# Windowed attention and a four-expert mixture in one schedule: rows of 512 bytes, weights in pieces, a third blocked group of batch 0, late rows through memory, and planner settings by phase

## The chip, the cores and the metric

The kernel runs on one core of one Trainium2 chip. The metric is the device time of one execution in microseconds, as a median of runs. The profile is of one further execution of the same program; its span goes from the first to the last instruction of the program.

The engines are named as in the profile: PE (TensorE, matrix products and, as PEld, weight loads), DVE (VectorE), ACT (ScalarE), POOL (GpSimd) and SP (SyncE). Each works through its own list of instructions in order. SP, ACT and POOL also issue transfers.

## The reference, cut to what matters

```python
# q, k, v: (4, 8, 768, 64) f32; n_sink 4, window 128
scores = q @ k.T / sqrt(64)
keep = (key < 4) | ((query - key >= 0) & (query - key < 128))
a = softmax(where(keep, scores, -1e9))
x = (a @ v) with the heads side by side        # (3072, 512)
# w1: (4, 512, 1024), w2: (4, 1024, 512), domain_probs: (3072, 4)
p = domain_probs / (domain_probs.sum(-1) + 1e-9)
out = sum over e of p[:, e] * (relu(x @ w1[e]) @ w2[e])   # (3072, 512) f32
```

So there is attention over a window of 128 keys and four sink keys, batch by batch, and behind it a mixture in which all four experts work on every token.

## The kernel before

**Units.** The 768 tokens of a batch are three groups `g` of 256. A unit is (batch `b`, group `g`, expert `e`). Attention of a group needs q and k with the head dimension on the partitions (`qkT`), scores per head pair (line 676, products of 64 rows), exponentials on ACT (702), masks on DVE (695, 711), the sinks' scores (637, 32 columns of weights at a time), the product with v (736, 743), a division (770 to 782) and a transpose into `xT`, on PE for batch 0 (801) and by a transfer on SP for the others (760).

**First product of a unit.** A slow unit has four steps of 8 products of 256 columns (1051); each needs a quarter of w1's columns. A fast unit does 7 block products instead of 8, each 8 products of 128 columns (1138), in the manner of Strassen and Winograd: DVE forms sums of weight blocks once per expert (`weight_form1`, 362) and of token blocks once per group (`tokens`, 1083), and per unit DVE adds two block results more than for a slow one (1191, 1206) and ACT copies two (1184, 1197). `START` says from which (batch, group) on an expert's units are fast. Results leave PSUM through relu for batch 0 (1064 to 1066, 1157 to 1159; the gate is applied after the second product), and through relu times gate on DVE for batches 1 to 3 (1075, 1171), which needs the gates spread over all partitions (`load_gate`, 453, a transfer on SP into one of `NGATE` = 5 buffers).

**Second product.** Batch 0's groups go through `emit_second` (1374): per half group and expert 8 products of 512 columns (1388), scaled and added by DVE (1398, 1400). The other nine groups, `PAIRS` (913), go by 7 block products for each of the four experts, summed over the experts in PSUM (`emit_product`, 1296; products of 256 columns at 1312), with block sums of the units' results formed by DVE (`chore`, 1215) and of w2 (`weight_form`, 326).

**Transfers in.** Batch 0's first group of q and k comes on SP and ACT as f32 (`load_first`, 254) and is cast (`cast_first`, 275). All other rows, v and the weights are cast by POOL's transfers: rows by `load_nat` (230; per 128 tokens one transfer of q and one of k, each with 1024 pieces of 256 bytes in memory) into `qkn` buffers, of which there are six; v by `load_v` (296), w1 by `load_w1` (306; expert 0 in two halves), w2 by `load_w2` (319). Batch 0 is turned on PE (`transposes`, 556), later batches by SP's transposing transfers (`turn_nat`, 241), six per batch, which can start when the scores of the batch before are done, since `qkT` has one buffer. `idle_products` (546) issues products of zeros where PE would stand idle.

**Order.** There is no scheduler at run time and none in the framework. The program's own planner sets the order while the kernel is built: it keeps a clock per engine in `t` (98), lists the steps that may come next with a time and a priority (main loop from 1446), emits the best, and keeps evictions in `pend` until their engine is due (`later`, `flush`, 142 to 165). The settings at lines 60 to 92 weigh the steps: `SHARE_OF`, `LEAD` and `DUE` how fast attention runs ahead of the mixture, `LOW_PRODUCT`, `LOW_SECOND`, `OPEN`, `EARLY` and `STEP0` the priorities, `GATE`, `FORM`, `TOKEN`, `MARGIN` and `MASK_SLACK` how long evictions and sums may wait, `PAIR` whether two scores steps go together, `FULL` and `WIDE` how many units are open. The transfers' place in their queues follows from the same loop (`loads`, `turns`).

```python
        opts.append((max(p, now), HIGH_PRODUCT if behind > BEHIND or mix.live >= FULL else LOW_PRODUCT, "product", None))
        opts += [(max(f, now), p, "first", x) for f, p, x in mix.firsts()]
        opts.append((max(s2, now), 1 if mix.since >= 1 else LOW_SECOND, "second", None))
        soonest = min(o[0] for o in opts)
        if soonest > now + 40 and flush(soonest, True):
            continue
        if soonest < 20000 and soonest > now + 220:
            idle_products(acc[1], 1, G)
            continue
```

The output is staged per group (`osb0`, `osb`, `osl`) and stored by SP. The last block product, P4 of the last group, is copied by ACT (1360) and stored by SP (1304).

Of the kernel before, what the change touches and what calls it, by code (L numbers as in the profile page):

```python
# [16 lines left out]
def kernel(  # L17
# [41 lines left out]

    NGATE = 5  # L60
    START = {0: (0, 2), 1: (0, 2), 2: (0, 0), 3: (2, 1)}
    MIX = 5
    SHARE_OF = (1.034, 1.037, 1.072)
    LEAD = (1.026, 0.9853)
    DUE = 1.356
    LOW_PRODUCT = 2.147
    LOW_SECOND = 2.509
    HIGH_PRODUCT = -1
    EARLY = 0.1973
    MASK_SLACK = 200.0  # L70
    GATE = 2639.0
    GATE0 = 6000.0
    FORM = 1000.0
    TOKEN = 4559.0
    MARGIN = 2117.0
    HOLD = 0
    FULL = 8
    STEP0 = 0.2923
    READY = 40
    WIDE = 3  # L80
    OPEN = 2.551
    ONACT = 1
    ONE = 2
    PAIR = 0
    BEHIND = 2351.0
    CHORES = 3
    OWN = 2
    LAST = 2
    BIASED = 1
# [8 lines left out]
    t = {"pe": 1200.0, "act": 0.0, "dve": 0.0, "pool": 1280.0, "sp": 800.0, "sw": 4800.0, "hw": 0.0}  # L98
    ring, whole = [0.0] * 6, [False] * 6
    WARM = 6600.0  # L100
    FLIP, LATE = 103.6, 500.0
# [79 lines left out]
    ROW = {64: 12.8, 128: 22.6, 512: 79.8, 1024: 156.2}  # L181

    def lands(key, rows, cols, *deps):
        issued = pool(0, *deps, fixed=880)
        at = max(t["sw"], issued + 1500)
        t["sw"] = at + rows * ROW[cols] / 16
        landed[key] = t["sw"] + 900 + (BACKLOG if key[0] == "w1" or backed else 0.0)
        if key[0] == "w1":
            backed.append(key)
        moved.append([key, at, t["sw"], ROW[cols]])  # L190

    moved, backed = [], []
    BACKLOG = 1300.0
    TURNED, SHARE = 66, 31.0

    def sp(*deps, issue=530, takes=600, turning=False):
        t["sp"] = max([t["sp"], *deps]) + issue
        at = max(t["hw"], t["sp"] + 800)
        row = next((x[3] for x in moved if x[1] <= at < x[2]), 0.0)
        if turning and row:  # L200
            t["hw"] = at + TURNED * (row + SHARE)
            t["sw"] += TURNED * SHARE
            for x in moved:
                if x[2] > at:
                    x[1] += TURNED * SHARE * (x[1] > at)
                    x[2] += TURNED * SHARE
                    landed[x[0]] = x[2] + 900 + BACKLOG * bool(backed)
                    if x[0][0] == "w1" and ("w1", x[0][1]) in landed:
                        landed["w1", x[0][1]] = max(landed["w1", x[0][1]], landed[x[0]])
        else:  # L210
            t["hw"] = at + takes + max(0.0, min(takes, t["sw"] - at)) * (not turning)
# [17 lines left out]

    def load_nat(b, tb):  # L230
        both = sb.tile([P, 2, H, D], BF16, name="qkn", tag="qkn", bufs=NQB)
# [9 lines left out]
    def turn_nat(b, tb):  # L241
# [8 lines left out]
        qkn_free.remove(1e12)  # L250
        qkn_free.append(turned_at[b, tb])
        qkn_free.sort()

    def load_first():

        raw = {name: mo.tile([P, 2, 4, 2 * D], FP32, name=f"{name}raw", tag=f"wide{i}", bufs=1) for i, name in enumerate("qk")}
        for half in range(2):
            hs = slice(4 * half, 4 * half + 4)
            for name, src in (("q", q), ("k", k)):
                x = raw[name][:, half]  # L260
                (nc.sync if name == "q" else nc.scalar).dma_start(
                    out=x, in_=src[0, hs, 0:G, :].rearrange("h (p t) d -> p h (t d)", t=2),
                )
                nat[0, half, name, "raw"] = x
            landed["first", half] = ((4870.0, 5180.0), (7550.0, 7350.0))[half]
# [5 lines left out]
    first = {name: sb.tile([P, 2, H, D], BF16, name="qkn", tag="qkn", bufs=NQB) for name in "qk"}  # L271
    qkn_free[-2:] = [1e12] * 2
    cast_at = {}

    def cast_first(half):
        hs = slice(4 * half, 4 * half + 4)

        def cast(at):
            cast_at[half] = at
# [1278 lines left out]
```

## Time and profile before

| | |
|---|---|
| runs | 361.69, 362.18 and 364.25 us; median 362.18 |
| profiled execution | 362.99 us, of which the span is 361.2 |
| PE, share of the span | 97% |
| weight loads | 82% |
| DVE | 82% |
| ACT, POOL | 46%, 19% |
| moved by transfers | 37.25 MB |
| POOL's queue (q0) | 77520 packets, 17.31 MB |
| SP's queue (q1) | 38668 packets, 18.75 MB |
| granted clock of PE | 1.00 |

The shares are busy time over the span. Busy intervals of consecutive instructions overlap, so a share near 100% says that the engine always had an instruction under way, not that it did its most. In the lines that follow, a group has busy time in us, the mean of one in ns, then the idle time before it and what ended that.

### The profile page before, as it was taken

The page shows a single profiled execution, that of the slowest core. Times are in us where ns is not written, and L with a number is a line of the kernel's source. Part 1 is how long each engine was busy: PE and PEld are TensorE (multiplying, and loading weights), DVE is VectorE, ACT ScalarE, POOL GpSimd, SP SyncE. Part 2 cuts the span into 40 slices and gives each one's busy share as a digit, 9 for nine tenths or more (in the row PEclk, how much of TensorE's full clock was granted, in tenths as well). Part 3 has the DMA queues.
Part 4 walks back from the last instruction along what each step waited for, and adds up shares of the span by engine and source line. Part 5 has one row for each costly group of instructions (what it writes and reads, how often), then busy time and mean ns, then how long its engine had stood idle before and what let it go on. Part 6 is the DMA issues. An engine that isn't in the chain of part 4 may idle for free.

```text
span 361.2 us, 10566 instructions
## 1 busy us (share of the span) xinstructions
PE 351.7 (97%) x4410; PEld 296.2 (82%) x4423; DVE 296.4 (82%) x671; ACT 164.9 (46%) x419; POOL 70.4 (19%) x90
## 2 busy tenths in 40 slices
PE   8799999998999999999999999999999999999996
PEld 3485767756668868898899899899999999999985
DVE  4665999868868979789789989979999998987840
ACT  5764634557754463655464465546222223212110
POOL 8935016223500616101440000000000000000000
PEclk9999999999999999999999999999999999999999
DMA  9999999999943999917899131214113102000011
GB/s 172 182 186 201 210 209 177 149 126 184 149 92 97 146 175 152 135 49 74 128 155 174 16 104 31 55 50 62 37 25 89 31 22 85 16 29 33 0 61 58
DMA packets 117292, 37.25 MB, mean 103 GB/s; under 512 B 100613, under 2 KB 112741, under 8 KB 117245
## 3 DMA queue, kind: packets, MB, share of 16 engines
q0 software_dynamic: 77520, 17.31, 56.1%
q1 hardware_dynamic: 38668, 18.75, 26.0%
q8 instruction: 34, 0.56, 0.6%
q10 hardware_dynamic: 1056, 0.52, 0.5%
q14 instruction: 14, 0.11, 0.2%
HBM read 40.45 MB, written 6.34 MB: 130 GB/s over the span
## 4 chain that ended last, share of the span: by engine, by line
PE 72%; DMA 21%; POOL 4%; issue 1%; DVE 1%; ACT 0%; SPq 0%
PE acc L1312 31%; PE cps L1138 27%; DMA w<-in_moe_w_dram 11%; PE hps L1051 6%; DMA qkn<-in_k_dram 4%; DMA vx<-in_v_dram 3%; PE acc L1388 3%; DMA xT<-onat 2%; PE sps L676 2%; PE od L743 2%; POOL qkn L233 1%; POOL vx L298 1%; PE od L736 1%; POOL w L311 1%; POOL w L321 0%
## 5 line engine op out<-in xcount | busy, mean ns | idle before, releaser
L1138 PEld LDWEIGHTS <-w 128*128 128x128 bf16 x1184 | 73.3, 98 | 3.7 <-issue 1.5
L1312 PEld LDWEIGHTS <-H 128*128 128x128 bf16 x600 | 56.0, 98 | 6.2 <-issue 0.6
L702 ACT ACTIVATE aT<-sps 128x512 bf16<-128x512 f32 (+1 forms) x96 | 47.4, 573 | 18.5 <-PE sps L676 18.5
L1171 DVE SCALAR_TENSOR_TENSOR H<-cps,gates 128x512 bf16<-128x512 f32 x78 | 52.9, 682 | 1.3 <-PE cps L1138 0.2
L1138 PEld LDWEIGHTS <-vf 128*128 128x128 bf16 x768 | 47.3, 98 | 1.7 <-issue 0.4
L1312 PE MATMUL acc<-w,H 128*128 128x256 bf16 x360 | 47.7, 273 | 0.0
L1138 PE MATMUL cps<-T,w 128*128 128x128 bf16 x592 | 45.1, 219 | 0.1
L1138 PE MATMUL cps<-xT,w 128*128 128x128 bf16 x592 | 44.8, 219 | 0.0
L1388 PE MATMUL acc<-w,H 128*128 128x512 bf16 x179 | 43.4, 379 | 1.0 <-issue 0.5
L782 ACT ACTIVATE onat<-od,R 128x64 bf16<-128x64 f32 x144 | 32.9, 324 | 23.9 <-DVE R L770 23.9
L1051 PE MATMUL hps<-xT,w 128*128 128x256 bf16 x352 | 43.5, 273 | 0.1
L1184 ACT COPY cps<-cps 128x512 f32<-128x512 f32 x37 | 21.4, 579 | 38.4 <-PE cps L1138 32.8
L1138 PE MATMUL cps<-T,vf 128*128 128x128 bf16 x512 | 38.3, 219 | 0.1
L1051 PEld LDWEIGHTS <-w 128*128 128x128 bf16 x352 | 32.9, 98 | 5.6 <-issue 1.3
L1388 PEld LDWEIGHTS <-H 128*128 128x128 bf16 x192 | 17.8, 98 | 17.9 <-issue 0.3
L298 POOL DMA_DIRECT2D vx<-in_v_dram x24 | 21.4, 901 | 48.8 <-PE od L743 44.8
L1312 PEld LDWEIGHTS <-S 128*128 128x128 bf16 x288 | 27.2, 98 | 2.9 <-issue 0.2
L1191 DVE TENSOR_TENSOR cps<-H,cps 128x512 f32<-128x512 f32 x31 | 21.4, 692 | 8.4 <-PE cps L1138 5.5
L1360 ACT COPY osb<-acc 128x256 f32<-128x256 f32 x28 | 10.5, 373 | 38.3 <-PE acc L1312 38.3
L1312 PE MATMUL acc<-wf,H 128*128 128x256 bf16 x184 | 25.8, 273 | 0.0
L695 DVE TENSOR_TENSOR aT<-aT,mask 128x1024 bf16<-128x1024 bf16 (+1 forms) x36 | 22.8, 640 | 1.9 <-ACT aT L702 1.7
L1206 DVE TENSOR_TENSOR H<-H,cps 128x512 f32<-128x512 f32 x31 | 21.2, 683 | 3.8 <-PE cps L1138 3.7
(126 smaller groups left out, 543.9 us busy)
## 6 DMA issues: line engine op xcount, KB each, us to landing
w<-in_moe_w_dram POOLq DMA_DIRECT2D x7, 1024.0 KB, 16.2
out_dram<-osb SPq DMA_DIRECT2D x19, 256.0 KB
gates<-gate_rows SPq DMA_DIRECT2D x36, 128.0 KB
vx<-in_v_dram POOLq DMA_DIRECT2D x24, 128.0 KB, 6.9
qkn<-in_q_dram POOLq DMA_DIRECT2D x22, 128.0 KB, 6.8
qkn<-in_k_dram POOLq DMA_DIRECT2D x22, 128.0 KB, 7.2
w<-in_moe_w_dram POOLq DMA_DIRECT2D x2, 512.0 KB, 9.0
out_dram<-osl SPq DMA_DIRECT2D x4, 256.0 KB
```

Of the source, the lines that this page charges most:

```text
L298: nc.gpsimd.dma_start(out=vx[tb][:, :, 0:D], in_=v[b, :, tb * P:(tb + 1) * P, :].rearrange("h p d -> p h d"),)
L695: nc.vector.tensor_mul(a, a, m[:, None, :].to_broadcast([P, 2, w]))
L702: nc.scalar.activation(out=a[:, ph], in_=sps[ph][:, 0:w], func=AF.Exp, scale=scale)
L782: nc.scalar.mul(o[:, qi, hp, ph * D:(ph + 1) * D], od[:, qi, ph, 0:D], R[:, qi, ph])
L1051: nc.tensor.matmul(h[:, i].rearrange("p (q n) -> p q n", q=2), lhsT=w1_sb[e][:, db, fb * P:(fb + 1) * P], rhs=xT[b, g][:, :, db], start=(i ...
L1138: nc.tensor.matmul(y[:, f], lhsT=A[:, d, f * P:(f + 1) * P], rhs=T[:, d], start=(m in ("P1", "P5") and f == 0 and d == 0), stop=(d == 1), ...
L1171: nc.vector.scalar_tensor_tensor(out=dst, in0=src, scalar=0.0, in1=gate, op0=ALU.max, op1=ALU.mult)
L1184: nc.scalar.copy(out=tiles["Y"], in_=y)
L1191: nc.vector.tensor_add(tiles["V"], c5, tiles["X"])
L1206: nc.vector.tensor_add(c5, c5, y)
L1312: nc.tensor.matmul(x, lhsT=self.operand(b, g, e, m)[:, f], rhs=forms[e][m][:, f], start=(k == 0 and f == 0 and m in (("P1", "P5", "P2") if ...
L1388: nc.tensor.matmul(op, lhsT=H[:, fb // QF, fb % QF, s], rhs=w2_sb[e][:, fb, :], start=(fb == 0), stop=(fb == NFB - 1),)
```

## The change

What it does, part by part:

- **Rows of 512 bytes.** Batch 0's groups 2 and 3 (`g` = 1, 2) are fetched with two neighbouring tokens per partition (`load_runs`), so that a piece in memory has 512 bytes; q and k of a group are one transfer each. The pairs are then regrouped by eight copies of 256 columns per group, q's on DVE and k's on ACT, in front of the transposes on PE; the copies out of PSUM put the tokens back in order. The first group's casts go by head pair instead of by half.
- **Weights in pieces.** Expert 0's w1 comes in quarters, and a step of the first product waits for its quarter alone; its w2 comes in two halves of 256 columns, and the second product with it goes by half columns.
- **Third group's second product in blocks.** Batch 0's third group joins `PAIRS`: its units are gated on eviction, like those of later batches, and it takes the 7 block products. For this the gate rows are made once the planner's clock passes `ROWS` and no longer when attention of batch 0 is done, and four more gates are loaded. The units of this group come in the order of the experts. `START` also moves: expert 0 is fast from batch 2 on instead of from batch 0's third group, expert 3 from (2, 0) instead of (2, 1).
- **Late rows through memory.** q and k of batches 2 and 3 are cast into a buffer in memory by POOL's transfers and turned from there by SP's, so that they need no `qkn` buffer.
- **Refitted by phase.** Most settings become four values, one for each stretch of the planner's clock (up to 60, 130 and 220 us, and behind), chosen by `by`. `PAIR` and `FORCE` can make scores steps wait for their partner.
- **Smaller ones.** The masks are built by other instructions and earlier, the zeros come first on DVE and the idle products ahead of the first rows are of 256 columns (13 written out, and more where the planner sees a wait), the sinks' v is loaded for batch 0 first, the last P4 is copied in halves by ACT and DVE and stored in halves by ACT and SP. The product of 512 columns that marks a fast unit's second PSUM bank as written (1144 to 1149) occurs twice in the new order and never in the old one.

The diff, cut to its core:

```diff
+    SPLIT = (60000.0, 130000.0, 220000.0)
-    START = {0: (0, 2), 1: (0, 2), 2: (0, 0), 3: (2, 1)}
+    START = {0: (2, 0), 1: (0, 2), 2: (0, 0), 3: (2, 0)}
-    SHARE_OF = (1.034, 1.037, 1.072)
-    LEAD = (1.026, 0.9853)
-    DUE = 1.356
+    SHARE_OF = (1.044, 0.95, 1.067)
+    LEAD = (1.012, 0.9701)
+    DUE = (1.063, 2.057, 1.149, 1.283)
-    GATE = 2639.0
+    GATE = (300.0, 1413.0, 1377.0, 471.2)
-    PAIR = 0
+    PAIR = (0, 1, 1, 1)
+    FORCE = (0, 0, 1, 1)
...
+    def by(x):
+        return x[sum(t["pe"] > at for at in SPLIT)]
...
     def load_nat(b, tb):
+        if b > 1:
+            if b not in turned_rows:
+                turned_rows[b] = dram.tile([S, 2, H, D], BF16, name=f"rows{b}")
+            x = nat[b, tb] = turned_rows[b][tb * P:(tb + 1) * P]
+            for i, src in enumerate((q, k)):
+                nc.gpsimd.dma_start(out=x[:, i], in_=src[b, :, tb * P:(tb + 1) * P, :].rearrange("h p d -> p h d"))
+                lands(("qk", b, tb), H * P, D)
+            return
...
+    def load_runs(g):
+        x = mo.tile([P, 2, H, 2, D], BF16, name="runs", tag="H" if g == 1 else "osb", bufs=NH if g == 1 else 1)
+        for i, src in enumerate((q, k)):
+            nc.gpsimd.dma_start(
+                out=x[:, i].rearrange("p h t d -> p h (t d)"),
+                in_=src[0, :, g * G:(g + 1) * G, :].rearrange("h (p t) d -> p h (t d)", t=2),
+            )
...
+        for hp in range(NHP):
+            part = join(2, lambda at, hp=hp: regrouped.__setitem__((g, hp), at))
+            for i, engine in enumerate(("dve", "act")):
+                def run(engine, i=i, h=2 * hp, part=part):
+                    copy(engine, rows[i][:, :, h:h + 2], x[:, i, h:h + 2].rearrange("p h t d -> p t h d"))
+                    part(clock(engine, 4 * D, rate=1.3))
+                later(engine, landed["qk", 0, g], 200 * hp, run)
...
-        nc.gpsimd.dma_start(out=w2_sb[e], in_=moe_w2[e].rearrange("(fb p) d -> p fb d", p=P))
+        for c in halves(e):
+            nc.gpsimd.dma_start(
+                out=w2_sb[e][:, :, c], in_=moe_w2[e][:, c].rearrange("(fb p) d -> p fb d", p=P),
+            )
...
-    for tb in (2, 3):
-        load_nat(0, tb)
-    load_v(0, (2, 3))
-    load_w1(0, 2, [0])
-    load_w1(0, 2, [1])
+    load_runs(1)
+    if not VPOS:
+        load_v(0, (2, 3))
+    load_w1(0, QF, [0, 1])
+    if VPOS:
+        load_v(0, (2, 3))
+    load_w1(0, QF, [2, 3])
...
             def run(engine):
-                copy(engine, dst, trs[0].rearrange("c i t p -> c i (t p)"))
+                copy(engine, dst.rearrange("c i (p t) -> c i p t", t=2), trs[0].rearrange("c i t p -> c i p t"))
...
-    PAIRS = [(b, g) for b in range(1, B) for g in range(NG)]
+    PAIRS = [(0, NG - 1)] + [(b, g) for b in range(1, B) for g in range(NG)]
...
-            self.early = {g: list(range(E)) for g in range(NG)}
+            self.early = {g: list(range(E)) for g in range(NG - 1)}
...
-            return max(free_at(), landed.get(("w1", e, 0), 1e12) if first else landed.get(("w1", e), 1e12), *xs)
+            return max(free_at(), landed.get(("w1", e, 0 if e else j), 1e12), *xs)
...
-                if b == 0:
-                    self.second += [(g, s, e) for s in range(2)]
+                if (b, g) not in PAIRS:
+                    self.second += [(g, s, e, c) for c in halves(e) for s in range(2)]
...
+            if final and m == CHAIN[-1]:
+                for i, engine in enumerate(("act", "dve")):
+                    c = slice(i * P, (i + 1) * P)
+                    copy(engine, C21[:, c], x[:, c])
+                    (nc.sync if i else nc.scalar).dma_start(out=out[r + P:r + 2 * P, c], in_=C21[:, c])
+                return
...
         now = t["pe"]
+        if now > ROWS and not rowed:
+            rowed.append(0)
+            gates_by_row()
+            load_gates()
...
+        hold = by(FORCE) and due and att.two() and max(turned(att.b, att.todo[0][3], *(att.todo[i][2] for i in range(2)))) < now and free_at(4) > now
+        opts += [(max(f, now), p, "first", x) for f, p, x in mix.firsts() if not (hold and x[0] in HELD)]
```

396 lines of the change are left out of this document (211 added, 185 removed).

## The prediction

> **What bounds the kernel now.** I read the engines' shares first, then the stretches of the span, then the chain that ended last, then TensorE's own waits and the program's order of instructions.
>
> ```profile
> span 361.2 us, 10566 instructions
> PE 351.7 (97%) x4410; PEld 296.2 (82%) x4423; DVE 296.4 (82%) x671; ACT 164.9 (46%) x419; POOL 70.4 (19%) x90
> PE   8799999998999999999999999999999999999996
> DMA  9999999999943999917899131214113102000011
> ```
>
> TensorE is busy to the end, so only its work and the places where it is not fed can move the time. By stretches (PE, weight loads, DVE, ACT, POOL; then clock, DMA, GB/s):
>
> ```profile
> 6.07:18.50 12.43, 10.21 (x143) 6.29 (x142) 8.30 (x29) 9.64 (x23) 12.03 (x18) 1.00 1.96 177
> 18.50:37.50 19.00, 18.79 (x195) 13.20 (x194) 11.09 (x33) 10.84 (x22) 7.87 (x10) 1.00 1.53 194
> 37.50:60.00 22.50, 22.26 (x231) 16.75 (x232) 21.93 (x45) 11.68 (x23) 6.72 (x8) 1.00 1.46 198
> 140.00:240.00 100.00, 99.93 (x1354) 89.29 (x1352) 89.22 (x207) 54.37 (x150) 15.36 (x18) 1.00 0.73 90
> 240.00:361.20 121.20, 118.05 (x1585) 111.32 (x1582) 99.34 (x209) 31.47 (x75) 0.00 (x0) 1.00 0.16 42
> ```
>
> Busy hides pipelining, so I laid the starts of successive products against what each takes back to back (16 of L1138 in 0.89 us, 8 of L1312 in 0.87, 8 of L1388 in 1.73). The program's products come to 334.8 us. The rest of the span: 1.4 until the first product, 5.8 of idle products (L549), 7.0 at 75 changes between 128-row products and the scores' 64-row or the sinks' 32-column ones (about 0.1 us each), some 9 of waits, 3.1 behind the last product. At 37.54, where the first product with the second expert's w1 starts, 24.2 us of real work are done, so 13.3 have been lost; from there to the last product's end at 358.05, 9.9 more. The early loss hangs on arrivals. The chain that ended last (start and length, us) runs over the weights' transfers until 55:
>
> ```profile
> 10.68 14.08 DMA w<-in_moe_w_dram
> 27.83 27.32 DMA w<-in_moe_w_dram
> ```
>
> and TensorE's timeline (start, busy, idle before it in brackets) shows who waits:
>
> ```profile
> 13.73 0.90 PE L570 MATMUL tr<-ident,qkn 128*128 128x128 bf16 x13 [1.15 <-DMA qkn<-in_k_dram]
> ...
> 17.33 0.39 PE L549 MATMUL acc<-lent 128*128 128x256 bf16 x2
> ...
> 18.52 0.27 PE L1051 MATMUL hps<-xT,w 128*128 128x256 bf16 x1
> ...
> 84.32 0.29 PE L637 MATMUL sinks<-qkT,ksd 128*32 128x256 bf16 x4 [0.80 <-DMA qkT<-qkn]
> ```
>
> The reader is to see that the second group's rows release TensorE at 13.73, dense work (L1051) begins only at 18.52, and one transfer wait of 0.8 us stands at 84.
>
> **TensorE's work: 0.** In the program's order L1051 gains 96 products of 256 columns (+10.5 us at 0.109), L1138 loses 168 of 128 (-9.3 at 0.0556), L1312 gains 112 of 256 (+12.2), L1388's 192 of 512 become 64 of 256 and 96 of 512 (-13.8), two seeds of 512 come in (+0.4). The sum is 0.0: what the third group saves by blocks is spent on three fewer fast units.
>
> **Before the first rows: 0 (0 to +1.0).** The idle products ahead of the first transposes shrink from 5632 to 4864 columns. They start every 0.427 us per 512 columns, half the later pace, and the pace doubles near 6.1. Should the slow pace last to 8, the 1.0 us of products in between would take twice as long; I take nothing, since the new ones begin 0.3 sooner and run without a break too. The masks are built by other instructions; DVE is done with such work at 3.9 and sits idle until the first cast at 4.67, which hides it.
>
> **The front: -1.6 (-2.3 to +0.5).** SP and ACT fetch the first rows as before; the casts come in quarters, which gains some 0.4 us up to the first scores, but those then wait for v at 8.53 and 9.44, as now. On POOL's queue the second group's four row loads become two. Seven loads of 128 KB landed from 8.53 to 14.69, 0.88 each. The two of 256 KB I put between two weights' rate (2.5 us for as many bytes) and no gain (3.5); between the packets seen (128 bytes 13.75 ns, 1024 bytes 78 ns, per engine share) 256 bytes take about 23 ns, so 1.47 each. The rows then land at 12.4 instead of 13.69. New behind them: four regroup copies on DVE for q and four on ACT for k (a 256-column copy starts every 0.23 and 0.27 us), and the copies out of PSUM write with a stride (L269's strided 256 columns took 416 ns on DVE against 285 plain, so some 0.26 more per half). ACT's four stand in front of its copies of the turned rows, DVE's in front of the last head pair's reciprocal: the transposes start near 12.9 and the first scores near 14.2, against 14.97. v lands at 14.1. w1 in quarters (42 ns by the same line, 1.34 us each) brings the first quarter at 15.45, where a half came at 17.16. In the new order L1051's first product stands right behind two scores, not behind four scores and two values. So dense work starts at 15.5. From there to the second expert's w1 the order holds 17.8 us of products, some 1.1 of changes, 0.45 for the gates' transposes: 34.8. That weight lands at about 34.6 (four row loads in place of eight and six pieces of weights in place of three shift the queue by only 0.2 from 34.79), so it just fits. Progress there is 23.1 us of work, 1.1 less than before at 37.54: 2.74 - 1.1 = 1.6. The halves of w2 (22.2 and 24.9) are asked for at 22.2 and 25.8. POOL issues about as many transfers (0.9 us each) and nobody waits for it.
>
> **Fewer changes of shape: -0.9 (0 to -0.9).** Behind that point the order has 47 changes instead of 56, at 0.096.
>
> **Later waits: -1.4 (from -3.5 to +1.5).** The sinks' wait of 0.87 between starts should go: those products stand some 7 us later in the order, while their rows are asked for no later. New on SP: gate loads for the third group, two of them waiting for a buffer between the second and third transpose of batch one; behind them stand four transposes, and batch one's sinks wait for those. I count that inside the bounds. The other 5.2 us of small waits are replanned with new settings; nothing before shows what each will be. I take -0.5, nearer to no change, since they were planned before as well.
>
> **Vector work: 0.** Rows give +16 gated evictions (682 ns), -8 reluing ones (4.9 us), -4.5 of second-product evictions, +16 of 416 for the blocks' operands, -6 of 690 for fast units, +8 regroup copies: about +6 us on 296. It is spread over 30 to 140 us, where DVE idles some 14 us; in 37 to 60, at 97%, relus and evictions leave as gates come. If that cover is gone, the excess is paid one for one.
>
> **The end: -0.15 (-0.4 to +0.2).** The last copy (0.37) is split between ACT and DVE and its transfer in two; behind the last product 3.1 us stay mostly transfer.
>
> **Late rows through memory: 0 (up to +15).** They no longer wait for buffers, but batches two and three are written to memory and turned from there. The transposes on SP take 1.3 us from buffers, 2.9 to 5.0 while row loads run. Between the last scores of a batch and the first of the next the order holds 8.3 and 10.6 us of other products (11.0 and 12.5 before): enough for two at 1.3 and their landing. I take no cost, the calm row being nearest.
> Here the Trainium skill speaks against the change: DMA: Bandwidth & Descriptors, "Why small descriptors are slow (HBM only)", puts a penalty on small pieces of memory and not on SBUF to SBUF, and these are pieces of 128 bytes. No run here shows it yet; by it the sum would be that of the slower rival below.
>
> **Sum.** The profiled execution took 362.99 for its span of 361.2, and stands 0.8 above the median of 362.18. Against its own time: 362.99 - 1.6 - 0.9 - 1.4 - 0.15 = 358.9; from the median, 358.1.
>
> **Rivals.**
> *The front's gain is eaten* (0.20): regrouping and strided copies cost what earlier rows bring, or the second expert's w1, which comes no earlier, holds TensorE. For: that weight lands within 0.2 us of when it is asked for. Against: the first quarter comes 1.7 us sooner. Without the 1.6 and the small replanned 0.5: 360.2.
> *The new settings take half of the small waits* (0.15): -2.6 in place of -0.5, so 356.0. For: there are settings for four phases now. Against: 0.09 us of waits were left behind 240, and many of the rest are 0.1 to 0.2 long.
> *Late rows are late* (0.08), the slower side: transposes from memory at 4.2 us, the mean of the three slow ones (2.9, 4.6, 5.0). Batch two's sinks need all six; about 16 us of products stand ahead of them from the last scores on, 13 of these left for issuing. 25.2 - 13 = 12 us stall, and 3 more in batch three (25.2 against 22): 373. It starts to cost at 2.2 us each and makes the kernel over 1% slower at about 3.5.
>
> **Chances.** The likeliest has 0.57, with its own range 356.4 to 360.0. About 1% (3.6 us, so below 358.6 or above 365.8) is what a measurement of this kernel can tell from no change. The likeliest lies just on the faster side: 0.36 of its 0.57 counts faster, 0.21 within; with the settings' rival faster is 0.51, with the eaten front within is 0.41, slower 0.08. The range, 354.8 to 361.8, leaves out the slow rival and about 0.1 at its ends.
>
> **What would show it.** Rows of the second group landing at about 12.4; dense work from 15.5; the second expert's w1 in use at about 35; no wait of the sinks near 90; SP's late transposes at 1.3 us; about 47 late changes of shape. I am wrong if TensorE waits for the regroup copies beyond 14, if a transfer wait opens at 34 to 36, or if DVE's share in 37 to 100 reaches 100% with TensorE waiting for it.

## The result, and the profile after

The changed kernel took 364.87 us (median of 18 runs, 363.92 to 367.88); the kernel before took 362.50 in the same comparisons. The ratio is 1.007 (1.0047 to 1.0093): slower by 0.7%, where 1% faster was forecast. The profiled execution took 364.15, its span 362.4, so against the profile before 1.2 us have to be found. The medians ask for 2.4, since the profile before stood 0.5 above its median and the one after stands 0.7 below.

The page of the changed kernel:

```profile
span 362.4 us, 10642 instructions
...
PE 353.1 (97%) x4449; PEld 307.6 (85%) x4449; DVE 301.5 (83%) x700; ACT 158.4 (44%) x417; POOL 68.6 (19%) x89
...
PE   8989999999989999999999999999999999999996
...
DMA  9999999999999217999992205203011111110011
```

Here are its stretches up to 60 us, and then two shorter ones that matter (from, to; length; busy PE, PEld, DVE, ACT, POOL; clock, DMA share, GB/s):

```profile
6.07:18.50 12.43, 11.96 (x153) 8.28 (x150) 10.91 (x34) 11.23 (x30) 11.60 (x18) 1.00 1.81 181
18.50:37.50 19.00, 17.91 (x210) 15.09 (x211) 13.57 (x43) 11.45 (x26) 7.18 (x9) 1.00 1.47 198
37.50:60.00 22.50, 21.80 (x208) 16.40 (x207) 20.53 (x44) 7.25 (x15) 4.81 (x6) 1.00 1.40 208
```

```profile
17.00:25.00 8.00, 6.58 (x86) 5.41 (x85) 6.31 (x23) 4.76 (x11) 3.36 (x5) 1.00 1.52 194
104.00:114.00 10.00, 8.33 (x98) 6.70 (x96) 7.60 (x22) 4.53 (x14) 1.69 (x2) 1.00 2.03 160
```

The same two in the kernel before:

```profile
17.00:25.00 8.00, 7.91 (x103) 6.71 (x103) 6.53 (x25) 5.84 (x12) 2.58 (x4) 1.00 1.47 196
104.00:114.00 10.00, 9.95 (x127) 7.57 (x126) 6.37 (x14) 4.17 (x17) 0.00 (x0) 1.00 0.22 81
```

Up to 18.50 us TensorE is fed better than before (11.96 us busy in place of 10.21). Then it loses 1.3 us between 17 and 25 and 1.6 between 104 and 114. These are TensorE's longest waits, first in the changed kernel, then in the kernel before (waiting group, releaser: us, times, longest); the first product's wait at the start is left out:

```profile
PE acc L1363 <- DVE S L1307: 1.6, 1, 1.6
...
PE tx L852 <- DVE onat L823: 1.1, 2, 0.7
PE od L793 <- DVE aT L761: 0.8, 2, 0.4
```

```profile
PE tr L570 <- DMA qkn<-in_k_dram: 1.1, 1, 1.1
PE sinks L637 <- DMA qkT<-qkn: 0.8, 1, 0.8
PE od L743 <- DVE aT L695: 0.7, 1, 0.7
```

The transfers' waits that the change was to shorten are gone; VectorE's have come in their place. The next table shows how much was lost at equal work. It takes the start of a product and subtracts what the products ahead of it take back to back, in us. The trace of before lacks some records, so its row is up to 0.65 too high from 26 on:

| work done, us | 6 | 8 | 12 | 23 | 26 | 85 | 95 | 140 | 330 |
|---|---|---|---|---|---|---|---|---|---|
| before | 11.9 | 12.0 | 12.1 | 13.4 | 13.5 | 17.5 | 17.5 | 20.6 | 23.8 |
| changed | 9.9 | 11.1 | 13.3 | 13.9 | 15.0 | 16.6 | 19.3 | 20.9 | 24.0 |

At 6 us of work (some 16 us into the span) the changed kernel is 2.0 ahead; at 12 (some 25 us into the span) it is 1.2 behind. It catches up until 85 us of work, since the sinks' wait is gone, and loses 2.7 in the next 10. This is what VectorE does where the first of it is lost, and below it TensorE's wait there:

```profile
15.33 1.01 DVE L1158 TENSOR_TENSOR T<-xT 128x256 bf16<-128x256 bf16 x1
16.46 0.29 DVE L1158 TENSOR_TENSOR T<-xT,T 128x256 bf16<-128x256 bf16 x1
16.67 0.42 DVE L761 TENSOR_TENSOR aT<-aT,mask 128x512 bf16<-128x512 bf16 x1
17.00 0.28 DVE L1158 TENSOR_TENSOR T<-xT 128x256 bf16<-128x256 bf16 x1
...
17.54 0.68 DVE L1117 TENSOR_SCALAR H<-hps 128x512 bf16<-128x512 f32 x1
18.14 0.75 DVE L761 TENSOR_TENSOR aT<-aT,mask 128x512 bf16<-128x512 bf16 x2
...
18.81 0.28 DVE L1158 TENSOR_TENSOR T<-xT,T 128x256 bf16<-128x256 bf16 x1
```

```profile
18.61 0.57 PE L793 MATMUL od<-vx,aT 128*128 128x65 bf16 x4 [0.44 <-DVE aT L761]
```

Four token sums (L1158) stand among the masks (L761) that TensorE waits for from 18.0 on. They belong to the first group's unit of the third expert, whose w1 lands at 44.8. Where the second part is lost, the chain that ended last runs over a store and not over an engine:

```profile
99.41 0.67 DVE osb L1467
...
100.09 6.18 DMA out_dram<-osb
```

```profile
103.51 0.42 DVE L1307 TENSOR_TENSOR S<-H 128x512 bf16<-128x512 bf16 x1
106.40 0.42 DVE L1307 TENSOR_TENSOR S<-S,H 128x512 bf16<-128x512 bf16 x1 [2.47 <-DMA out_dram<-osb]
```

```profile
106.88 0.61 PE L1363 MATMUL acc<-wf,S 128*128 128x256 bf16 x4 [1.56 <-DVE S L1307]
```

The third group's second block sums (`S1`, tag `wide1`) take the buffer from which the second group's output is stored. The store of 256 KB takes 6.18 us until it has landed, VectorE stands idle for 2.47, and TensorE waits for the sums from 105.3 to 106.9.

### The profile page after: what moved, and what is told of

It reads as the page before. It is cut to its first block, busy times and chain, and to the rows that moved or that the text cites. A ratio compares the mean times of both kernels' runs of the same rounds, so it can differ in the third digit from the quotient of the medians.

```text
span 362.4 us, 10642 instructions
## 1 busy us (share of the span) xinstructions
PE 353.1 (97%) x4449; PEld 307.6 (85%) x4449; DVE 301.5 (83%) x700; ACT 158.4 (44%) x417; POOL 68.6 (19%) x89
## 4 chain that ended last, share of the span: by engine, by line
PE 79%; DVE 10%; DMA 6%; ACT 3%; issue 1%; ACTq 0%; DVEq 0%
PE acc L1363 30%; PE cps L1189 27%; PE hps L1102 10%; PE acc L1453 6%; DMA xT<-onat 2%; PE od L793 2%; PE sps L726 2%; DMA out_dram<-osb 2%; DMA raw<-in_k_dram 2%; ACT onat L832 1%; DVE aT L745 1%; ACT aT L752 1%; DVE S L1307 1%; DVE aT L761 1%; DVE T L1158 1%; DVE H L1126 1%
## 5 line engine op out<-in xcount | busy, mean ns | idle before, releaser
L1363 PEld LDWEIGHTS <-H 128*128 128x128 bf16 x680 | 63.9, 98 | 7.6 <-issue 0.6
L1189 PEld LDWEIGHTS <-w 128*128 128x128 bf16 x1088 | 67.1, 98 | 2.1 <-issue 0.7
L1102 PE MATMUL hps<-xT,w 128*128 128x256 bf16 x448 | 55.5, 273 | 0.0
L1363 PE MATMUL acc<-w,H 128*128 128x256 bf16 x408 | 53.2, 273 | 0.0
L1102 PEld LDWEIGHTS <-w 128*128 128x128 bf16 x448 | 42.5, 98 | 6.9 <-issue 0.7
L1189 PEld LDWEIGHTS <-vf 128*128 128x128 bf16 x672 | 41.2, 98 | 1.0 <-issue 0.2
L1189 PE MATMUL cps<-T,w 128*128 128x128 bf16 x544 | 40.9, 219 | 0.1
L1189 PE MATMUL cps<-xT,w 128*128 128x128 bf16 x544 | 40.7, 219 | 0.0
L832 ACT ACTIVATE onat<-od,R 128x64 bf16<-128x64 f32 x144 | 32.7, 356 | 17.5 <-DVE R L820 17.3
L1189 PE MATMUL cps<-T,vf 128*128 128x128 bf16 x448 | 32.4, 219 | 0.0
L1453 PE MATMUL acc<-w,H 128*128 128x512 bf16 (+1 forms) x160 | 31.0, 337 | 0.0
L745 DVE TENSOR_TENSOR aT<-aT,mask 128x1024 bf16<-128x1024 bf16 (+1 forms) x36 | 22.8, 639 | 5.0 <-ACT aT L752 5.0
L1242 DVE TENSOR_TENSOR cps<-H,cps 128x512 f32<-128x512 f32 x28 | 19.3, 690 | 7.6 <-PE cps L1189 7.0
L1418 ACT COPY osb<-acc 128x256 f32<-128x256 f32 x28 | 11.1, 398 | 33.1 <-PE acc L1363 33.1
L1126 DVE SCALAR_TENSOR_TENSOR H<-hps,gates 128x512 bf16<-128x512 f32 x32 | 21.6, 681 | 3.2 <-PE hps L1102 3.1
L1453 PEld LDWEIGHTS <-H 128*128 128x128 bf16 x160 | 15.1, 98 | 10.1 <-issue 0.6
## 6 DMA issues: line engine op xcount, KB each, us to landing
w<-in_moe_w_dram POOLq DMA_DIRECT2D x6, 1024.0 KB, 20.9
```

Source lines behind the costliest of these rows:

```text
L745: nc.vector.tensor_mul(a, a, m[:, None, :].to_broadcast([P, 2, w]))
L832: nc.scalar.mul(o[:, qi, hp, ph * D:(ph + 1) * D], od[:, qi, ph, 0:D], R[:, qi, ph])
L1102: nc.tensor.matmul(h[:, i].rearrange("p (q n) -> p q n", q=2), lhsT=w1_sb[e][:, db, fb * P:(fb + 1) * P], rhs=xT[b, g][:, :, db], start=(i ...
L1126: nc.vector.scalar_tensor_tensor(out=dst, in0=h, scalar=0.0, in1=gate, op0=ALU.max, op1=ALU.mult,)
L1189: nc.tensor.matmul(y[:, f], lhsT=A[:, d, f * P:(f + 1) * P], rhs=T[:, d], start=(m in ("P1", "P5") and f == 0 and d == 0), stop=(d == 1), ...
L1242: nc.vector.tensor_add(tiles["V"], c5, tiles["X"])
```

## The experiments

Unless said otherwise, each is the changed kernel with TensorE's order unchanged: only the named instructions move on their own queue, and the planner's clocks still count them at the old place. The experiments were run in groups, each beside runs of the kernel before. The ratio in brackets is to those (with its 95% interval), so between two groups the ratios say more than the microseconds.

**The token sums** behind 23 us.

```diff
-                nc.vector.tensor_sub(*steps.pop(0))
+                x = steps.pop(0)
+                if n or t["pe"] > 24000:
+                    nc.vector.tensor_sub(*x)
+                else:
+                    sums.append(x)
...
         now = t["pe"]
+        while sums and now > 24000:
+            nc.vector.tensor_sub(*sums.pop(0))
```

> The changed kernel with one thing moved: the four token sums of batch 0's first group (first use behind 40 us) leave VectorE's queue at 15 to 19 us and stand behind 23 us instead; TensorE's order and every other engine's are held. Theory (VectorE's queue gives the front's gain back): the first mask starts at about 15.7 in place of 16.67, TensorE's waits of 0.60, 0.27 and 0.31 us at 17.96, 18.65 and 20.04 shrink to 0.3 in all, and the time falls by about 0.9 us to some 364.0 of the changed kernel's median of 364.9. Rival (the new order exposes each chain of values, division and turn, whoever is ahead in the queue): the same waits stay, 364.9. Rival (the difference is in the granted clock): 364.9 too.

363.51 us (ratio to before 1.0035, 1.002 to 1.0051): 1.4 less than 364.87, more than the 0.9 expected; 0.3 of it is the changed kernel's runs at a lower clock (below; the other twelve have a median of 364.59). The waits at 18 to 20 shrink from 1.18 to 0.64, and 0.7 us is kept at 25. But the first mask, which took 0.42 in the changed kernel, now takes 1.46 of the 1.80 in the first line below:

```profile
15.36 1.80 DVE L761 TENSOR_TENSOR aT<-aT,mask 128x512 bf16<-128x512 bf16 x2 [0.24 <-ACT aT L752]
```

```profile
15.48 1.05 POOL L665 TENSOR_TENSOR vsd<-vsf,sel 128x520 bf16<-128x520 f32 x1
```

The two masks take 1.80 together, where two in a row otherwise take 0.75. POOL's product (L665) runs beside them. In the changed kernel a token sum stood beside it and took 1.01 in place of 0.28; now it is a mask.

**The last two stores by ScalarE**, and, separately, **batch two's rows later**.

```diff
-                nc.sync.dma_start(out=out[r:r + P, :], in_=out_sb[g][:, s])
+                (nc.scalar if len(self.stored) > 1 else nc.sync).dma_start(out=out[r:r + P, :], in_=out_sb[g][:, s])
```

> The changed kernel with the last two stores of batch 0's staged output issued by ScalarE instead of SP; the orders of TensorE, VectorE and POOL are held. Theory (the wait of 1.72 us at 105 is a buffer: the third group's second block sums take the buffer from which group two's output is stored, and that store stands on SP's queue behind a turning transfer issued at 95.17 whose packets move from 97.9 to 102.0): the store's packets move at about 101 in place of 104.8 to 105.9, the wait shrinks to under 0.5, and the time falls by 1.3 to about 363.6. Rival (the rows of batch two fill the transfer engines, whatever the queue): the store lands as late, 364.9. Rival (VectorE itself is late with the sums): the wait stays, 364.9. If ScalarE is held by the store's wait on VectorE, some tenths come on top.

365.49 us (1.0083, 1.0068 to 1.0099). The theory had the wrong place: SP's queue is not what holds the store. Issued by ScalarE at 101.88, its packets still moved only from 106.2 to 107.3, and the wait was 1.59. ScalarE was held by the first store's wait for VectorE, and that cost TensorE another 1.07 at 101.6.

```diff
             for i, src in enumerate((q, k)):
-                nc.gpsimd.dma_start(out=x[:, i], in_=src[b, :, tb * P:(tb + 1) * P, :].rearrange("h p d -> p h d"))
+                def issue(x=x, i=i, src=src):
+                    nc.gpsimd.dma_start(out=x[:, i], in_=src[b, :, tb * P:(tb + 1) * P, :].rearrange("h p d -> p h d"))
+                deferred.append(issue) if b == 2 else issue()
...
             x[0](*x[1:])
+            while x[:2] == (load_v, 2) and deferred:
+                deferred.pop(0)()
```

> The changed kernel with the twelve row loads of batch two (q and k, written to memory) put behind the next load of v on POOL's queue, so that they start at about 104 instead of 91.5; every other order is held. Theory (the rows' packets of 128 bytes slow the turning transfer issued at 95.17, and the store behind it with it): the turning transfer is done by 97 instead of 102, the store's packets by 102 instead of 105.9, the wait at 105 goes, and the time falls by about 1.5, to 363.4, if the next turning transfer, which then meets the rows, costs nothing. Rival (SP's queue alone makes the store late): as before, 364.9. Against both: batch two's own transposes at 136 to 145 may come late, then up to 367.

363.84 us (1.0039, 1.0027 to 1.0052), 1.0 less. The first load of v waits for less than I thought: the rows still started at 95.3, and the transfer that turns `xT` on SP's queue and both stores still ran beside them (packets to 99.8, 103.1 and 105.9). The wait was 1.41 in place of 1.72, which does not decide between theory and rival. So the rows went behind all three loads of v (`while x == (load_v, 2, (2,)) and deferred`):

> As the kernel with batch two's rows later, but they stand behind all three of the next loads of v, the last of which waits for the values of batch one: they start at about 105 instead of 95.3 (there) or 91.5 (changed kernel). Orders of TensorE, VectorE, ScalarE and SP are those of the changed kernel. Theory (transfers that run beside batch two's rows are slow, and the third group's block sums wait for one of them): the turning transfer issued at 95.2 is done by 97.5, the two stores issued at 97.5 and 100.1 by 99 and 101.5, TensorE's wait of 1.72 at 105 shrinks below 0.3, and the time falls to about 363.0 of 364.9, since then the clock does not fall there either. Rival (a store takes that long by itself): the wait stays at 1.4 or more. Against: the next turning transfer, issued at 109.3, meets the rows; its landing then decides when batch one's second group starts, and up to 2 us could come back at about 115.

362.03 us (0.9993, 0.9983 to 1.0004): 2.8 less than the changed kernel, and the kernel before is reached. With no rows beside it the turning transfer's 1024 packets ran from 97.4 to 98.8 (97.6 to 101.9 in the changed kernel), the last store's from 101.4 to 102.2 (104.8 to 105.9), and the sums and their products follow without a wait:

```profile
103.95 0.42 DVE L1309 TENSOR_TENSOR S<-H 128x512 bf16<-128x512 bf16 x1
104.41 0.42 DVE L1309 TENSOR_TENSOR S<-S,H 128x512 bf16<-128x512 bf16 x1
```

```profile
104.74 1.04 PE L1104 MATMUL hps<-xT,w 128*128 128x256 bf16 x8
105.61 0.60 PE L1365 MATMUL acc<-wf,S 128*128 128x256 bf16 x4
```

So the late rows did cost, but not in their transposes from memory: these held SP for 1.24 to 1.86 us each in batch two and for 1.23 to 2.38 in batch three (1.3 was forecast), and no wait of TensorE hangs on them. They cost because, without a buffer to wait for, all twelve of batch two start one after the other from 91.5 on, beside a turning transfer and two stores whose buffer is needed at once. Before, six of them started from 87.6 on and the other six from 118.9.

**The clock.** The mean granted clock of six of the changed kernel's 18 runs is 0.993 to 0.995, and these are the runs of 366.2 to 367.9. None of these six was traced, but the profiled execution with the sums later is such a run (0.995); the clock is the third figure from the end:

```profile
104.00:106.00 2.00, 0.65 (x6) 0.33 (x4) 0.00 (x0) 0.38 (x1) 0.97 (x2) 1.00 1.93 225
106.00:108.00 2.00, 1.25 (x11) 1.13 (x12) 1.73 (x6) 0.84 (x4) 0.00 (x0) 0.76 2.43 155
108.00:110.00 2.00, 2.00 (x18) 1.75 (x16) 2.00 (x8) 1.48 (x6) 0.00 (x0) 0.50 2.43 154
110.00:112.00 2.00, 2.00 (x23) 1.67 (x22) 2.00 (x6) 0.38 (x1) 0.00 (x0) 0.88 1.88 128
```

Behind a wait of 2.27 us (counted between the starts of products) the clock is at half: of the three windows of 2 us the shares 0.24, 0.50 and 0.12 are missing, so 1.7 us of work, over 3.4 us. With w1 in halves (below) the wait was 2.35, and all five runs were at 0.995. Waits of 1.41 to 2.16 at this place left the profiled execution at 0.998 or more. So the wait at 105 costs 1.4 to 2.4, and in some runs 1.7 on top. The Trainium skill, TensorE: Matmul & The Clock Gate, "What's actually happening", has the clock halve after an idle window of some 3.4 us and come back after a busy one of the same length. The 3.4 us at half agree; the wait that set it off was only 2.3 here.

**Both moves**, sums and rows:

> Both at once: the first group's token sums behind 23 us, and batch two's rows behind the loads of v. Theory: the two losses are separate (the front's and the one at 105) and add up: the sums alone took the time to 363.5, the rows alone are to take 1.7 off, so 361.6 to 362.0, below the 362.5 of the kernel before. Rival (they are one loss, seen twice): 363.2.

360.95 us (0.9956, 0.9943 to 0.9968), 0.7 below the expected 361.6 to 362.0. The losses are separate, and without them the changed kernel is faster than the one before.

**What pieces and rows bring.** Batch 0's second group with 256-byte pieces and no regroup copies, and w1 in two halves:

```diff
+            if g == 1:
+                for tt in range(2):
+                    nc.gpsimd.dma_start(out=rows[i][:, tt], in_=src[0, :, (2 * g + tt) * P:(2 * g + tt + 1) * P, :].rearrange("h p d -> p h d"))
```

> The changed kernel with batch 0's second group fetched as before: four loads with pieces of 256 bytes for the two of 512, no regroup copies, plain copies out of PSUM; the planner is told nothing, so every order is held. Theory (the front's gain is the earlier rows, and its loss VectorE's queue): rows land at about 13.7 in place of 11.6, so the group's transposes start 0.4 to 0.6 later than at 13.28, but VectorE is freed of 0.9 us of copies and of 0.5 by plain ones, so the waits at 18 to 20 shrink; +0.5 - 0.6, the time stays within 0.5 of 364.9. Rival (the 512-byte rows carry the front's gain of 2 us): +1.5, 366.4. Rival (regroup and strided copies are what ate the gain): -1.0, 363.9.

364.47 us (1.0049, 1.0036 to 1.0062), as the theory had it. At 6 us of work it is 0.42 behind the changed kernel, and 0.26 from 12 on. That is all that the larger rows bring once the regroup and strided copies are paid for.

```diff
-            nc.gpsimd.dma_start(
-                out=w1_sb[e][:, :, i * n:(i + 1) * n],
+            c = slice(i * n, (i + 2) * n) if parts > 1 else slice(0, F)
+            if i % 2 == 0:
+                nc.gpsimd.dma_start(out=w1_sb[e][:, :, c], in_=moe_w1[e][:, c].rearrange("(db p) f -> p db f", p=P))
```

> The changed kernel with the first expert's w1 fetched in two halves instead of four quarters; the planner is told nothing, so every order is held. Theory: the first product with w1, which started at 15.18 behind a quarter landed at 14.80, waits for a half that lands at about 16.5, and the products between 15.2 and 24 slip by up to 1.3; since that stretch then loses 2.5 us to VectorE's queue anyway, about half of it is paid: +0.6, 365.5. Rival (the quarters make the front's gain): +1.3 or more, 366.2. Rival (quarters gain nothing behind VectorE's queue): 364.9.

366.70 us (1.0113, 1.0096 to 1.013). The median hides what quarters are worth, since the whole excess arises at 105, from the wait of 2.35 there and the clock behind it. In the front TensorE waits 1.32 for the half,

```profile
16.45 0.61 PE L1101 MATMUL hps<-xT,w 128*128 128x256 bf16 x4 [1.32 <-DMA w<-in_moe_w_dram]
```

and is 1.26 behind the changed kernel at 6 us of work, 0.38 at 8, and 0.00 at 10: both reach that mark at 21.71 us. So the quarters' whole gain is gone 5 us later, since the masks and the products with v behind it come no earlier.

**Two more losses of this kind.** In the changed kernel the gate rows are made earlier, since the third group is gated: four instructions of VectorE in one piece, in front of the third group's masks.

```profile
36.00 0.67 DVE L483 TENSOR_REDUCE scratch<-scratch 24x128 f32<-24x512 f32 x1
...
37.93 1.08 DVE L486 TENSOR_TENSOR scratch<-scratch 24x512 f32<-24x512 f32 x1
38.93 0.74 DVE L761 TENSOR_TENSOR aT<-aT,mask 128x512 bf16<-128x512 bf16 x2
```

And at 22.8 the order has nothing on TensorE between a group's last product with v, its division and its transpose. The next two experiments move one of these each; from here on the two moves above are always in.

```diff
+    row_steps = [
+        (20500, lambda: nc.vector.reduce_sum(out=ds, in_=dp, axis=AX.X)),
+        (27000, lambda: nc.vector.tensor_scalar_add(out=ds, in0=ds, scalar1=1e-9)),
+        (27000, lambda: nc.vector.reciprocal(out=ds, in_=ds)),
...
+        while row_steps and now > row_steps[0][0]:
+            row_steps.pop(0)[1]()
```

```diff
+        last = (b, hp, g) == (0, NHP - 1, 1)
+        turned_last.append(products) if last else products()
...
                     gates()
+                    while turned_last:
+                        turned_last.pop()()
```

> The kernel with the token sums and batch two's rows moved (360.95 us), and one thing more: the four instructions on VectorE that make the gate rows (3.0 us in one piece from 36.0 to 39.0 in the changed kernel, ahead of group three's masks, since the third group is gated now) go to idle places of VectorE at 21, 27 and 29 us; all else is held. Theory (a third loss of the same kind: TensorE's waits of 0.54 at 38.8 for a mask and 0.49 at 40.4 for a division are these instructions): both go, -0.9, 360.1. Rival (those waits are the chain of values, division and turn itself): they stay, 360.95. If a piece lands in front of something late, some of it comes back at 27 to 31.

360.22 us (0.9941, 0.9928 to 0.9954): 0.7 less than 360.95, 0.5 by the ratios, whose intervals overlap. Both waits (0.54 and 0.49) are gone from the trace, so they were these instructions and no bare chain.

> The kernel with the token sums and batch two's rows moved (360.95 us), and two neighbours on TensorE exchanged: the four small transposes of the domain probabilities stand in front of the last turn of the second group, not behind it. Theory (the wait of 0.90 at 22.8 is a bare chain, values, division, turn, with nothing in between on TensorE): the 0.65 us of transposes fit into it, -0.6, 360.35. Rival (VectorE or ScalarE is late there for another reason, and the next product waits for it instead): 360.95.

360.46 us (0.9943, 0.9929 to 0.9957): 0.5 less, with intervals that overlap too; of the wait of 0.90 there 0.42 stays.

**The sink values earlier**, POOL's product between the quarters of w1:

```diff
+    nc.gpsimd.tensor_mul(vsd[0], vsf[:, 0, None, None, :].to_broadcast([P, NHP, 2, DX]), sel2[:, :, :, None].to_broadcast([P, NHP, 2, DX]))
     load_w1(0, QF, [2, 3])
```

> The kernel with the token sums and batch two's rows moved (360.95 us), and one instruction of POOL put earlier: the product that spreads batch 0's sink values (1.06 us, at 15.1 to 16.7 in every trace so far) runs between the first expert's w1 quarters at about 9. In the changed kernel a token sum of VectorE that began beside it took 1.02 us in place of 0.28, and with the sums moved the first mask took 1.46 in place of 0.42: VectorE's instruction ends just after POOL's in both. Theory (the two engines do not work at the same time on such operands): the first mask takes 0.42, the masks behind it come 1.0 earlier, and TensorE's waits between 16 and 20 shrink; -0.4, 360.55, as little else is left to wait for there. Rival (a slow first use of the mask): the first mask takes 1.4 again, 360.95. Against: the third quarter of w1 is asked for 1 us later and may hold TensorE at about 18, up to +0.5.

365.58 us (1.0094, 1.007 to 1.0118), 4.6 more. Its input, the sinks' v from SP's queue, lands far later than the place supposes:

```profile
12.99 1.06 POOL L596 TENSOR_TENSOR vsd<-vsf,sel 128x520 bf16<-128x520 f32 x1 [4.12 <-DMA vsf<-in_v_dram]
```

POOL stood for 4.12 us with all its transfers behind it. TensorE waited 3.23, until 19.3, for the sinks' keys, which are POOL's work too, and the clock fell (0.991 to 0.995 in all runs). Yet the run settles what stretched the mask: with POOL's product out of the way the first two masks took 0.91 together, where they had taken 1.80. All five moves at once inherit the wait:

> All five moves at once: token sums, batch two's rows, gate rows, the last turn of the second group and the sink values. Theory (five separate losses that add up): 360.95 - 0.9 - 0.6 - 0.4 = 359.05. Rival (the second expert's w1, which lands at 34.6 and is no earlier, takes over when the front gets faster): TensorE waits for it at about 34 and no more than 0.5 is kept of the front's part, 359.7.

363.88 us (1.0043, 1.0027 to 1.0058). TensorE waits 2.69 for the sinks' keys, and the clock is at 0.991 to 0.995 in all runs. The trace also shows what POOL's product does not stretch, a division whose one operand (`od`) lies in PSUM:

```profile
12.58 1.06 POOL L599 TENSOR_TENSOR vsd<-vsf,sel 128x520 bf16<-128x520 f32 x1 [3.72 <-DVE R L831]
12.61 0.42 DVE L834 TENSOR_TENSOR onat<-od,R 128x256 bf16<-128x256 f32 x1
```

**Four moves**, without the sink values, and what quarters and rows are worth beside them:

> Four moves at once (token sums behind 23 us, batch two's rows behind the loads of v, gate rows to idle places of VectorE, small transposes ahead of the last turn of the second group); batch 0's sink values stay where the changed kernel has them. Theory (four separate losses that add up): 360.95 - 0.73 - 0.49 = 359.7. Rival (the second expert's w1, landed at 34.6, or another transfer takes over when the front gets faster): 360.2, with a new wait of TensorE between 30 and 40.

359.80 us (0.9934, 0.9917 to 0.9952), the best of all: 5.1 less than the changed kernel (4.9 by the ratios) and 2.3 less than the kernel before in the same comparison. The losses add up to what was expected. The longest of TensorE's waits is now in the front:

```profile
PE hps L1113 <- DMA w<-in_moe_w_dram: 1.4, 2, 1.0
```

It is the first expert's w1 again (1.4, in two waits at 14.8 and 16.7), not the second's, which the rival named.

> The four moves, and the first expert's w1 in two halves instead of four quarters. In the changed kernel the halves cost 1.26 us up to 17 us and nothing any more from 21.7 on, since VectorE's queue held TensorE there in any case. Theory (with that queue relieved the quarters' gain is kept): 0.6 to 1.2 slower than with quarters, 360.3 to 360.9. Rival (the chain of masks, values and turns holds that stretch still): the same time as with quarters, 359.7.

361.75 us (0.9992, 0.9974 to 1.0009). In the two profiles the halves cost 1.6 at 6 us of work, and 0.7 of it stays to the end: once VectorE's queue is relieved, the quarters' gain is kept in part. The runs spread from 360.17 to 363.43, and three of the twelve are at a clock of 0.995, so the 1.95 between the medians is not all the price of halves.

> The four moves, and batch 0's second group by loads with pieces of 256 bytes, without regroup copies, orders held. In the changed kernel this cost 0.26 us at 25 us. Theory (with the queue relieved the earlier rows count in full): rows 1.5 to 2 later, the group's transposes 0.4 later, so 0.4 slower than with 512 bytes, 360.1. Rival (the regroup and strided copies cost as much as the rows bring): 359.7.

360.30 us (0.9952, 0.9936 to 0.9969): 0.5 more, with intervals that overlap, and 0.2 in the profiles. The larger rows are worth no more than that.

**The old end**, one copy and one store:

```diff
-                for i, engine in enumerate(("act", "dve")):
...
+                nc.scalar.copy(out=C21, in_=x)
+                store(0.0, slice(0, G))
```

> The changed kernel with the end as it was before: the last 256 columns are copied by ScalarE in one piece and stored by one transfer on SP. From the last product's start to the end of the span the changed kernel took 3.70 us and the kernel before 3.39. Theory (the split costs what it looks like): -0.3 us, 364.6. Rival (the end is the store's completion, which varies by that much): 364.9 and 3.7 us again.

364.44 us (1.0055, 1.0039 to 1.0071), and the span ends 3.69 us behind the last product's start, as with the split (3.70; 3.39 before). The split neither costs nor gains. Most of the 0.3 lies in the waits with which SP closes the program, 0.06 each: behind the one that the last landing releases there is one more in the kernel before, and there are five here and four in the changed kernel.

## Why the prediction was wrong

- **The front, -1.6.** The gain was there: 2.0 at 6 us of work, dense work from 15.18 (forecast 15.5), rows landing at 11.6 (12.4). The experiments split it: some 1.3 comes from the quarters and 0.4 from the rows; the rest was not tried. But by the forecast 11.7 us were to be lost at 23.1 us of work, and 13.9 were. The step that failed is the reckoning from dense work at 15.5 to "34.8", in which the order holds "17.8 us of products, some 1.1 of changes, 0.45" and nothing waits in between. It put in regroup and strided copies, and left out what else stands in VectorE's queue by 19 us: four token sums, one of them stretched by POOL's product from 0.28 to 1.01, and a relu. With the sums out of the way 0.7 us came back there. It also left out that a first product moved ahead leaves less to cover the chain of mask, product with v, division and transpose behind it (the wait of 0.90 at 22.8). The second expert's w1 landed at 34.6 as forecast and was asked for at 37.0.
- **Vector work, 0.** The sum was right (301.5 for 296.4), the place was not: a total of busy time, and the idle 14 us from 30 to 140, do not say what is queued behind the gate rows. They stood at 41.2, behind the masks, and moved to 36.0, in front of them. That made 1.0 us of waits, and 0.5 to 0.7 us of the time.
- **Later waits, -1.4.** This is the second step that failed. The sinks' wait is gone, as forecast, and so is one of 0.84 at 128. But the new one of 1.4 to 2.4 at 105 was in no term. The third group's blocks take a buffer that a store must leave first; this is to be read from the tags in the code, and no view of before could have shown it.
- **Late rows through memory, 0.** Right about the transposes, so the rival of 373 was out. But "they no longer wait for buffers" stood there without a price, and the rows that start at once are what makes that store late: moving them brought 2.8 us, the clock included. The penalty that the Trainium skill, DMA: Bandwidth & Descriptors, "Why small descriptors are slow (HBM only)", puts on small pieces was not seen in batch two's transposes (1.24 to 1.86 us from memory, 1.23 to 1.81 from buffers before), nor in the loads, of which 128 KB landed every 0.85 us as into buffers before. Batch three's last three took 2.13 to 2.38, but they ran beside loads of v.
- **Changes of shape, -0.9:** 67 changes in place of 75, some 6.3 us against 7.0, so -0.7. **The end, -0.15:** +0.3.
- The rival "the front's gain is eaten" was right that nothing of the gain is left, but for the wrong reasons: neither the copies nor the second expert's w1 ate it. Its 360.2 is 4.7 us too low, since no rival had a wait at a buffer.

The four moves give 359.8, within the forecast range. The forecast thus came near to what the change can bring, without what its order takes back. That is loose support only: the range is 7 us wide, and the kernel with the moves is another one.

## What to carry to other kernels

When dense work is moved forward, read the queue of the engine that serves what is left behind it, instruction by instruction: what has its first use tens of microseconds later does not belong in front of a mask. Where a buffer changes hands through a store, it is free when the store has landed, beside whatever else then moves, and not when the store is issued. A load that no longer waits for its own buffer starts at once and may be the one in the way. And a long wait of TensorE, 2.3 us here, can have a second price, in the clock.

## What the runs showed of the hardware

- A turning transfer of 1024 packets took 1.4 us of transfer time with the rows out of the way and 4.3 in the changed kernel, beside row loads with pieces of 128 bytes, though those took only 0.85 us per 128 KB. Part of the 4.3 is a stop: both transfers all but cease from 99.75 to 101. The rates of 94 to 104, in quarters of a microsecond, have 45, 8, 6, 8 and 10 there:

```profile
GB/s 156 231 406 394 219 112 128 133 133 134 148 151 150 158 153 155 155 158 157 124 156 233 130 45 8 6 8 10 113 183 172 161 155 167 186 282 325 323 227 157
```

  An instruction fetch of 16 KB began at 99.4 and took 0.96 us; whether it is the cause was not tried. The stop does not need the rows: with them behind all loads of v a store all but ceases too, beside such a fetch from 98.6 to 99.7 (8, 8, 25 and 16 from 99.75 on):

```profile
GB/s 311 385 336 17 0 0 0 0 6 33 51 113 148 176 236 225 224 288 136 216 336 369 74 8 8 25 16 0 0 180 393 385 90 0 0 0 0 0 0 0
```

  Nor is it there beside every fetch: with the rows behind the first load of v one ran from 98.9 to 100.6, and no such gap came.
- A VectorE instruction with both operands in SBUF that ran beside POOL's 128x520 product ended only 0.15 to 0.3 us after it: a sum took 1.01 us in place of 0.28, a mask 1.46 in place of 0.42, and 0.42 again with that product elsewhere. The division with one operand in PSUM took its 0.42 beside it. The Trainium skill, GPSIMD Engine Reference, in its first table, names the shared interface and instructions with two SBUF inputs; this agrees.
- A TensorE wait of 2.3 us was enough for half the clock over 3.4 us; waits of up to 2.16 at the same place were not, in the executions traced.
